# Linear attention and a top-1 expert layer on one core: two halves of a tile get PSUM banks of their own, a transpose moves from TensorE to VectorE, and four smaller edits

## The chip, the core and the metric

The kernel runs on one core of one Trainium2 chip. The metric is the device time of one execution in microseconds (us). TensorE multiplies and transposes into PSUM; VectorE (DVE), ScalarE (ACT) and GpSimd (POOL) work element by element; SyncE (SP) only issues transfers, and ACT issues a few too. Each engine runs its own instructions strictly in order, and an instruction starts when the semaphores that it waits for have reached their values.

## The reference

```python
def phi(x):                                   # 128 random features
    proj = np.einsum('bhsd,md->bhsm', x, omega)
    h = proj - np.sum(x * x, axis=-1, keepdims=True) / 2.0
    return np.exp(h - np.max(h, axis=-1, keepdims=True)) / np.sqrt(m)
q_p, k_p = phi(q_s), phi(k_s)                 # 4 batches, 8 heads, 576 rows, 64 columns
kv = np.einsum('bhsm,bhsd->bhmd', k_p, v); z = np.sum(k_p, axis=2)
x = np.einsum('bhsm,bhmd->bhsd', q_p, kv) / (np.einsum('bhsm,bhm->bhs', q_p, z)[..., None] + 1e-06)
# x as 2304 rows of 512; then a top-1 expert layer, 8 experts, at most 576 rows each
logits = x @ w_gate; e = argmax(logits); gate = softmax(logits)[e]
y[e] = relu(rows_of_e @ w1[e]) @ w2[e]        # 512 -> 1024 -> 512
out[i] = gate[i] * y[e][place of i]           # 0 where row i found no place
```

## The kernel before

**The attention.** The k phase has 18 steps n. Each projects 4 key units (`pjk`, line 172, TensorE), takes their maxima (`mx`, line 189, DVE), and makes the exponentials of the first half of the step on ACT out of PSUM (`ex`, line 794) and those of the second half by a DVE add (line 800) and an ACT exponential (line 803). Two steps later TensorE adds `ex` times v into `kacc` or `kp` (line 239). In step n=1 both halves lie in one tile of two banks (`x = pair("pjk1")`); from n=2 on each half has a bank of its own. When a batch's half is complete, the generator `kv_gate` copies it out, transposes it with two small pairs of TensorE transposes (`ktr`, line 264), which take the bank called SM, copies them on ACT (`kvT`, line 268) and multiplies by the gate weights (line 277). Its `yield "E"` hands over to the end of the running step.

**The q phase** has 18 tiles t and three steps behind them: project (`pjq`), subtract the maxima (`d`: ACT lines 809 and 827, POOL line 813), transpose (`qtr`, line 763), exponentiate (`qpT`, ACT line 819), multiply by kv (`qacc`, line 648), divide on DVE (`normalise`) and store the rows to the scratch tensor `x_d`. In steps 5 to 8 the transposes of the first 256 rows of expert item 0 (`xtri`, bank SM) run between those of `qtr`.

**The expert items.** A block of 576 rows goes through one expert: `mm1` for each of 8 column blocks f and two halves (rows 0 to 255, rows 256 to 575) with 12 matmuls in high and low parts (lines 689 to 691), evacuated by ACT (`hhi`, line 696; `hf`, line 698) and DVE (`hlo`, line 699) out of three banks in turn; then `mm2_rest` for the last 64 rows and `mm2` for four tiles of 128 rows (lines 866 to 868), `finish` (scale by the gate on ACT, line 896) and `put`, the store to `out` (line 930). `put` issues four of an item's five stores from SP and the last, the fourth 128-row tile, from ACT. Item 0 always runs; of the others, behind branches, items 1 and 2 run with this data, and item 3 does not. The rows of a later item and its w1 are loaded by `prefetch` in the item before, its w2 after the item's first `mm1`. Rows of items 1 and 2 are turned by a DVE transpose in `turn_x` (lines 402 to 406). Rows 256 to 575 of item 0 are instead turned by TensorE in three groups (line 412), one ahead of each of the last three half-0 column blocks f = 3, 4, 5, each followed by an ACT cast (line 422) and a DVE subtract (line 424).

**What sets the order.** Each engine's instructions stand in the order of the code; tiles in rotating buffers make the waits. All plain transfers go through eight counting semaphores, named DMAHW0 to DMAHW7 in the orders below.

Of the kernel before, what the change touches and what calls it, by code (L numbers as in the profile page):

```python
# [9 lines left out]
F32 = mybir.dt.float32  # L10
# [12 lines left out]
NT = N // 128  # L23
# [40 lines left out]
def attention_moe(ctx, tc, kT, qT, va, om, wg, w1, w2, cap, ident, tri, desc, lst, tab0, out):  # L64
# [183 lines left out]
    def kv_gate(b, g, acc):  # L248
        kv = kv_sb[b][:, 4 * g : 4 * g + 4, :]
        yield "E"  # L250
        nc.vector.tensor_copy(kv[:, :, 0:VW], acc[:, 0 : 4 * VW].rearrange("p (h c) -> p h c", h=4))
        kvc = small.tile([128, 2 * M], F32, tag="kvc", name=f"kvc{b}{g}", bufs=2)
        nc.scalar.copy(kvc.rearrange("p (h c) -> p h c", h=4), kv[:, :, 0:D])
        yield "E"
        kvT = small.tile([128, 2 * M], F32, tag="kvT", name=f"kvT{b}{g}", bufs=2)

        for a in range(2):
            f = slice(64 * a, 64 * a + 64)
            tr = []

            def small_t():
                tr.append(bank(SM, f"ktr{b}{g}{a}"))
                for i in range(2):
                    nc.tensor.transpose(tr[0][:, i * 64 : (i + 1) * 64], kvc[f, i * M : (i + 1) * M], id_sb[f, f])

            beside.append((a, small_t))
            yield "T"
            nc.scalar.copy(
                kvT.rearrange("p (i m) -> p i m", i=2)[:, :, f], tr[0][:, 0:128].rearrange("p (i m) -> p i m", i=2)
            )  # L270
        yield "T"
# [12 lines left out]
        yield "E"  # L284
        nc.vector.tensor_copy(kv[:, :, VW:ROW], sm[:, 0 : 4 * E].rearrange("p (h c) -> p h c", h=4))
# [33 lines left out]
    def setup():  # L319
# [5 lines left out]
        yield from pause(12)  # L325
        nc.vector.tensor_copy(cap_f, cap_i[:, 0:1])
        nc.vector.tensor_copy(tri_b, tri_sb)
        nc.vector.memset(ones_b, 1.0)
        nc.gpsimd.memset(sc_b, 0.0)
# [36 lines left out]

    def load_w(i, c, ev, chunks_of="(k p)"):
        if i == 1:
# [24 lines left out]

    def load_x(row):
        src = x_d[ds(row, SLOTS), :].rearrange("(b r) (q c) -> q r b c", r=32, q=4)
        for q in range(4):
            nc.sync.dma_start(big["xz"][32 * q : 32 * q + 32, :, :], src[q])


    def turn_x(b0, b1):  # L400
        t = big["xt"][:, 0 : b1 - b0, :].rearrange("p b (k r) -> p b k r", k=4)
        nc.vector.transpose(t, big["xz"][:, b0:b1, :].rearrange("p b (a k) -> p b k a", k=4))
        t = t.rearrange("p b k r -> p k b r")
        hi, lo = (big[x][:, :, 32 * b0 : 32 * b1].rearrange("p k (b r) -> p k b r", r=32) for x in ("xhi", "xlo"))
        nc.scalar.copy(hi, t)
        nc.vector.tensor_tensor(lo, t, hi.bitcast(F32), op=ALU.subtract)

# [231 lines left out]
    def first_rows():  # L639
        nc.sync.dma_start(  # L640
            big["xg"][:, 2:, :], x_d[2 * SUB : NSUB * SUB, :].rearrange("(i p) d -> p i d", p=SUB)
        )

# [14 lines left out]
    def normalise(t, acc):  # L658
        xr = small.tile([128, ROW, H], F32, tag="xr", name=f"xr{t}", bufs=4)
        if t < 2:  # L660
            xr_l[t] = xr
        av = acc.rearrange("p (i x) -> p i x", i=2)[:, :, 0 : NP * ROW].rearrange("p i (h c) -> p c i h", c=ROW)
# [10 lines left out]
        nc.vector.tensor_reduce(lg[:, t, :], xr[:, D + 1 : ROW, :], op=ALU.add, axis=AX.X)  # L673
        nc.sync.dma_start(x_d[t * 128 : (t + 1) * 128, :], xr[:, 0:D, :].rearrange("p c h -> p (c h)"))

    HALVES = [(0, 256), (256, SLOTS)]
# [42 lines left out]
    for n in range(NK + NT + 3):  # L719
# [3 lines left out]
        if n < NK:  # L723
# [6 lines left out]
            else:  # L730

                x = pair(f"pjk{n}") if n == 1 else None
                pj = [bank(2 * (n % 2) + i, f"pjk{n}{i}") if n > 1 else x[:, 512 * i : 512 * i + 512] for i in range(2)]
                project(keys, pj)
# [7 lines left out]
        if 0 <= t - 2 < NT:  # L742
# [7 lines left out]
            if t in FIRST_AT:  # L750
# [3 lines left out]
                rows = slice(64 * i, 64 * i + 64)  # L754
                x0 = xr_l[k0 // 2][:, 0:D, :].rearrange("p c h -> p (c h)")
                parts[i][0:0] = [
                    (tr[:, k * 64 : (k + 1) * 64], x0[rows, k * 128 : (k + 1) * 128], i) for k in range(4)
                ]
# [47 lines left out]
        else:  # L806
# [15 lines left out]
            if t >= NT:  # L822

                take()
            if t < NT:
                for k in range(4):
# [4 lines left out]
            if 0 <= t - 3 < NT:  # L831
                normalise(t - 3, acc_l[0])
                if t == 3:
                    start(first_item())
            run(times=3)
        if 0 <= t < NT and t - QB[c] == 2 and c + 2 < len(QB) - 1:
# [50 lines left out]

    def finish(i, pt, nm, scale, put):
        n = sub_n[i]
        y = hpool.tile([SUB, DM], F32, tag="y", name=f"ys{nm}{i}", bufs=3)  # L890
        src = pt
        if n < SUB:
            src = y
            nc.scalar.copy(y[0:n, :], pt[n : 2 * n, :])
            nc.vector.tensor_tensor(y[0:n, :], pt[0:n, :], y[0:n, :], op=ALU.add)
        nc.scalar.mul(y[0:n, :], src[0:n, :], scale[0:n])
        put(i, n, y)

# [18 lines left out]
    def item(j):  # L917
# [8 lines left out]

        def put(i, n, y, out_j=out_j):

            k = int(i == NSUB - 2)
            (nc.sync, nc.scalar)[k].dma_start(out_j[k][i * SUB : i * SUB + n, :], y[0:n, :])  # L930

        def prefetch():
# [4 lines left out]
            row = nc.sync.value_load(resd[0:1, 1, j : j + 1], min_val=0, max_val=N - S)  # L937
            load_x(row)
            for c in range(4):
                load_w(1, c, ev, "(p k)")  # L940
            evs.append(ev)
# [3 lines left out]
        for k, (f, half) in enumerate(STEPS[j > 0]):  # L945

            if j == 0 and k < 3:
                for _ in transpose_x(2 + k, nm, (SM, 3, None)[k]):
                    pass
            mm1(f, half, hhi, hlo, hf, nm)()  # L950
            if j == 0:

                listing(5 if k > 2 else 1)
            if j > 0 and k == 0:
                for c in range(4):
# [15 lines left out]
        for n, i in enumerate((NSUB - 1, *range(NSUB - 1))):  # L971
            pt = mm2(i, hhi, hlo, nm) if n > 0 else mm2_rest(hf, nm)
            finish(i, pt, nm, sc[:, i : i + 1], put)
            yield

            if not last:
                if n == 1:
                    turn_x(0, NBA)
                for c in ((), (0,), (1,), (), ())[n]:
                    split_w_hi(1, c)  # L980
                    split_w_lo(1, c)
                if n == 2:
                    turn_x(NBA, NB)

# [63 lines left out]

    def put_rows(i, n, y):
        scatter(out, idx[0:n, i, 0:1], y[0:n, :], N - 1)  # L1050
# [8 lines left out]
    with ExitStack() as ifs:  # L1059
# [5 lines left out]
        for j in range(J):  # L1065
# [5 lines left out]
            for c in range(4):  # L1071
                load_w(1, c, ev)
            for c in range(4):
# [81 lines left out]
```

## Time and profile before

| what | value |
|---|---|
| median of 3 runs | 266.65 us (265.68 to 266.78) |
| profiled execution, its own time | 265.75 us |
| span of its profile | 263.9 us, so 1.85 us lie outside the span |
| TensorE busy in the span | 254.9 us, 97% |
| DVE, ACT, POOL busy | 163.5, 149.0 and 36.7 us |
| granted TensorE clock | 0.994 of full speed |

The profiled execution is 0.9 us below the median. The busy share of TensorE is an average: it does not tell in which stretch it waits, so the stretches around each edit have to be read one by one.

### The profile page before, as it was taken

The page shows a single profiled execution, that of the slowest core. Times are in us where ns is not written, and L with a number is a line of the kernel's source. Part 1 is how long each engine was busy: PE and PEld are TensorE (multiplying, and loading weights), DVE is VectorE, ACT ScalarE, POOL GpSimd, SP SyncE. Part 2 cuts the span into 40 slices and gives each one's busy share as a digit, 9 for nine tenths or more (in the row PEclk, how much of TensorE's full clock was granted, in tenths as well). Part 3 has the DMA queues.
Part 4 walks back from the last instruction along what each step waited for, and adds up shares of the span by engine and source line. Part 5 has one row for each costly group of instructions (what it writes and reads, how often), then busy time and mean ns, then how long its engine had stood idle before and what let it go on. Part 6 is the DMA issues. An engine that isn't in the chain of part 4 may idle for free.

```text
span 263.9 us, 7550 instructions
## 1 busy us (share of the span) xinstructions
PE 254.9 (97%) x3070; PEld 226.6 (86%) x3070; DVE 163.5 (62%) x327; ACT 149.0 (56%) x375; POOL 36.7 (14%) x54
## 2 busy tenths in 40 slices
PE   7899999999999999999999999999999999999991
PEld 6789999999899999999868789996788999958880
DVE  3899888779989985745764725553337064633550
ACT  4688887999989993436413415552252255424321
POOL 2010000333469893000000000000000000000000
PEclk9999999999999999999999999999999999999997
DMA  7999760045867667791079439990011999101111
GB/s 226 390 383 330 273 230 2 5 156 166 275 214 234 248 251 260 256 387 67 2 144 292 170 87 348 190 283 1 21 42 48 292 263 298 36 2 53 46 42 45
DMA packets 33187, 46.56 MB, mean 176 GB/s; under 512 B 2227, under 2 KB 22067, under 8 KB 33139
## 3 DMA queue, kind: packets, MB, share of 16 engines
q1 hardware_dynamic: 32018, 44.42, 53.6%
q10 hardware_dynamic: 1120, 1.52, 1.7%
q8 instruction: 28, 0.46, 0.7%
q14 instruction: 21, 0.16, 0.2%
HBM read 34.00 MB, written 11.93 MB: 174 GB/s over the span
## 4 chain that ended last, share of the span: by engine, by line
PE 85%; DVE 5%; DMA 3%; ACT 2%; issue 2%; DVEq 0%
PE hi L689 10%; PE hi L690 10%; PE hi L691 10%; PE yi L866 8%; PE yi L867 8%; PE yi L868 8%; PE qacc L648 6%; PE pjq L172 5%; PE pjk L172 5%; DVE mx L189 3%; PE kacc L239 3%; DMA qraw<-qT 3%; PE kp L239 3%; PE qtr L763 3%; DVE ex L800 1%
## 5 line engine op out<-in xcount | busy, mean ns | idle before, releaser
L689 PE MATMUL hi<-xhi,w1hi 128*128 128x256 f32 (+1 forms) x192 | 57.1, 297 | 0.0
L690 PE MATMUL hi<-xhi,w1lo 128*128 128x256 f32 (+1 forms) x192 | 56.4, 294 | 0.0
L691 PE MATMUL hi<-xlo,w1hi 128*128 128x256 f32 (+1 forms) x192 | 56.3, 293 | 0.0
L699 DVE SCALAR_TENSOR_TENSOR hlo<-hi,hhi 128x256 fp32r<-128x256 f32 x48 | 20.2, 421 | 40.8 <-ACT hf L698 22.6
L696 ACT ACTIVATE hhi<-hi 128x256 fp32r<-128x256 f32 x48 | 18.5, 385 | 37.2 <-PE hi L691 37.2
L866 PE MATMUL yi<-w2hi,hhi 128*128 128x512 f32 x96 | 37.8, 393 | 0.1
L867 PE MATMUL yi<-w2hi,hlo 128*128 128x512 f32 x96 | 37.4, 389 | 0.0
L868 PE MATMUL yi<-w2lo,hhi 128*128 128x512 f32 x96 | 37.4, 389 | 0.0
L689 PEld LDWEIGHTS hi<-xhi,w1hi 128*128 128x128 f32 x192 | 36.0, 188 | 0.4
L690 PEld LDWEIGHTS hi<-xhi,w1lo 128*128 128x128 f32 x192 | 36.0, 188 | 0.1
L691 PEld LDWEIGHTS hi<-xlo,w1hi 128*128 128x128 f32 x192 | 36.0, 187 | 0.0
L813 POOL TENSOR_TENSOR d<-d,mx 128x512 f32<-128x512 f32 x18 | 18.7, 1041 | 53.1 <-DVE mx L189 49.6
L189 DVE TENSOR_REDUCE mx<-pjk 128x4 f32<-128x512 f32 (+1 forms) x38 | 23.3, 653 | 4.5 <-PE pjk L172 3.2
L866 PEld LDWEIGHTS yi<-w2hi,hhi 128*128 128x128 f32 x96 | 18.0, 188 | 6.5 <-issue 2.9
L794 ACT ACTIVATE ex<-pjk,mx 128x128 f32<-128x128 f32 x72 | 20.7, 369 | 4.8 <-DVE mx L189 4.6
L172 PE MATMUL pjk<-om_s,kraw 64*128 64x128 f32 x288 | 22.6, 287 | 0.7 <-DMA kraw<-kT 0.5
L648 PE MATMUL qacc<-kv_sb,qpT 128*64 128x73 f32 x576 | 22.4, 229 | 0.2 <-DVE e L601 0.2
L172 PE MATMUL pjq<-om_s,qraw 64*128 64x128 f32 x288 | 21.3, 284 | 0.5 <-DMA qraw<-qT 0.4
L868 PEld LDWEIGHTS yi<-w2lo,hhi 128*128 128x128 f32 x96 | 18.0, 188 | 3.8
L648 PEld LDWEIGHTS qacc<-kv_sb,qpT 128*64 128x64 f32 x576 | 19.8, 136 | 1.6 <-PE qtr L763 0.3
L867 PEld LDWEIGHTS yi<-w2hi,hlo 128*128 128x128 f32 x96 | 18.0, 188 | 3.6
L827 ACT ACTIVATE d<-pjq,mx 128x128 f32<-128x128 f32 x72 | 21.1, 405 | 0.1
(141 smaller groups left out, 399.4 us busy)
## 6 DMA issues: line engine op xcount, KB each, us to landing
w1raw<-w SPq DMA_DIRECT2D x16, 512.0 KB, 8.2
w2raw<-w SPq DMA_DIRECT2D x12, 512.0 KB, 4.9
qraw<-qT SPq DMA_DIRECT2D x6, 768.0 KB, 6.8
x_d<-xr SPq DMA_DIRECT2D x18, 256.0 KB, 3.2
v<-va SPq DMA_DIRECT2D x7, 650.0 KB, 6.7
xg<-x_d SPq DMA_DIRECT2D x12, 288.0 KB, 7.2
out<-zero_sb SPq DMA_DIRECT2D x4, 768.0 KB, 6.4
kraw<-kT SPq DMA_DIRECT2D x5, 576.0 KB, 6.5
```

The costliest lines, as they stand in the source:

```text
L172: nc.tensor.matmul(banks[i][:, k * M : (k + 1) * M], parts[k][rows, :], om_s[rows, :], start=True, stop=True)
L189: nc.vector.tensor_reduce(mx[:, a : a + src.shape[1]], src, op=ALU.max, axis=AX.X, negate=True)
L648: nc.tensor.matmul(acc[r : r + 64, i * 512 + p * ROW : i * 512 + (p + 1) * ROW], qpT[:, r // 64, (4 * i + p) * 64 : (4 * i + p) * 64 + 64] ...
L689: nc.tensor.matmul(pt, whi_[:, k, fs], xhi[:, k, sl], start=(k == 0), stop=False)
L690: nc.tensor.matmul(pt, wlo_[:, k, fs], xhi[:, k, sl], start=False, stop=False)
L691: nc.tensor.matmul(pt, whi_[:, k, fs], xlo[:, k, sl], start=False, stop=(k == 3))
L699: nc.vector.scalar_tensor_tensor(hlo[:, f, sl], pt[:, 0:w], 0.0, hhi[:, f, sl].bitcast(F32), op0=ALU.max, op1=ALU.subtract)
L794: nc.scalar.activation(ex[:, o + k, :], q[0][:, k * M : (k + 1) * M], AF.Exp, bias=mx[:, o + k : o + k + 1], scale=1.0)
L827: nc.scalar.activation(d[:, 4 + k, :], pj[1][:, k * M : (k + 1) * M], AF.Identity, bias=mx[:, 4 + k : 5 + k], scale=1.0)
L866: nc.tensor.matmul(pt, hhi[:, f, sl], w2hi, start=(f == 0), stop=False)
L867: nc.tensor.matmul(pt, hlo[:, f, sl], w2hi, start=False, stop=False)
L868: nc.tensor.matmul(pt, hhi[:, f, sl], w2lo, start=False, stop=(f == 7))
```

## The change

1. `kv_gate`: one more `yield "E"`; the transposes, copies and gate matmuls of each batch half come one step later.
2. `setup`: two small casts and a memset go from DVE to POOL.
3. w1 of item 0 is loaded in the other chunk order, POOL copies the first two `normalise` results into the buffer `xt` in that order, and the extra transposes of the q phase read `xt`.
4. Rows 256 to 575 of item 0 are loaded by four transfers in the layout of `turn_x` and turned by two DVE transposes of 128x640 in steps t=18 and 19, each followed one step later by an ACT cast and a POOL subtract of 128x4x160. The three groups of TensorE transposes, ACT casts and DVE subtracts are gone.
5. In step n=1 the first half goes to the bank SM, the second to the first bank of the pair.
6. The w2 of item 3 is loaded in item 2 behind its second store; the w2 loads of items 0 to 2 stay.
7. `finish` scales the fourth tile in two halves of 256 columns, and `put` stores the first half from SP, the second from ACT.

```diff
@@ kv_gate
         nc.scalar.copy(kvc.rearrange("p (h c) -> p h c", h=4), kv[:, :, 0:D])
         yield "E"
+        yield "E"
@@ setup
-        nc.vector.tensor_copy(cap_f, cap_i[:, 0:1])
-        nc.vector.tensor_copy(tri_b, tri_sb)
-        nc.vector.memset(ones_b, 1.0)
+        nc.gpsimd.tensor_copy(cap_f, cap_i[:, 0:1])
+        nc.gpsimd.tensor_copy(tri_b, tri_sb)
+        nc.gpsimd.memset(ones_b, 1.0)
@@
-    def load_w(i, c, ev, chunks_of="(k p)"):
+    def load_w(i, c, ev, chunks_of="(p k)"):
@@
-    def load_x(row):
-        src = x_d[ds(row, SLOTS), :].rearrange("(b r) (q c) -> q r b c", r=32, q=4)
+    def load_x(rows, b0=0):
+        src = x_d[rows, :].rearrange("(b r) (q c) -> q r b c", r=32, q=4)
         for q in range(4):
-            nc.sync.dma_start(big["xz"][32 * q : 32 * q + 32, :, :], src[q])
+            nc.sync.dma_start(big["xz"][32 * q : 32 * q + 32, b0:, :], src[q])
-    def turn_x(b0, b1):
-        t = big["xt"][:, 0 : b1 - b0, :].rearrange("p b (k r) -> p b k r", k=4)
+    def turn_x(b0, b1, o=0, eng=nc.vector):
+        t = big["xt"][:, o : o + b1 - b0, :].rearrange("p b (k r) -> p b k r", k=4)
         nc.vector.transpose(t, big["xz"][:, b0:b1, :].rearrange("p b (a k) -> p b k a", k=4))
...
-        nc.scalar.copy(hi, t)
-        nc.vector.tensor_tensor(lo, t, hi.bitcast(F32), op=ALU.subtract)
+        def split():
+            nc.scalar.copy(hi, t)
+            eng.tensor_tensor(lo, t, hi.bitcast(F32), op=ALU.subtract)
+
+        return split
@@ first_rows
-        nc.sync.dma_start(
-            big["xg"][:, 2:, :], x_d[2 * SUB : NSUB * SUB, :].rearrange("(i p) d -> p i d", p=SUB)
-        )
+        load_x(slice(32 * NBA, SLOTS), NBA)
@@ normalise
+        if t < 2:
+            xr_l[t] = big["xt"][:, 4 * t : 4 * t + 4, :]
+            nc.gpsimd.tensor_copy(xr_l[t], xr[:, 0:D, :].rearrange("p c h -> p (c h)").rearrange("p (m k) -> p k m", k=4))
@@ the k phase
-                x = pair(f"pjk{n}") if n == 1 else None
-                pj = [bank(2 * (n % 2) + i, f"pjk{n}{i}") if n > 1 else x[:, 512 * i : 512 * i + 512] for i in range(2)]
+                if n == 1:
+                    pj = [bank(SM, "pjk10"), pair("pjk11")[:, 0:512]]
+                else:
+                    pj = [bank(2 * (n % 2) + i, f"pjk{n}{i}") for i in range(2)]
@@ the q phase
+            if t > NT:
+                split_x()
...
+            if t in (NT, NT + 1):
+                b0 = NBA + 5 * (t - NT)
+                split_x = turn_x(b0, b0 + 5, b0 - NBA, nc.gpsimd)
@@ finish
-        nc.scalar.mul(y[0:n, :], src[0:n, :], scale[0:n])
-        put(i, n, y)
+        w = DM // parts
+        for c in range(0, DM, w):
+            nc.scalar.mul(y[0:n, c : c + w], src[0:n, c : c + w], scale[0:n])
+            put(i, n, y, c, w)
@@ put
-            k = int(i == NSUB - 2)
-            (nc.sync, nc.scalar)[k].dma_start(out_j[k][i * SUB : i * SUB + n, :], y[0:n, :])
+            k = int(i == NSUB - 2 and c > 0)
+            (nc.sync, nc.scalar)[k].dma_start(out_j[k][i * SUB : i * SUB + n, c : c + w], y[0:n, c : c + w])
@@ item
-            if j == 0 and k < 3:
-                for _ in transpose_x(2 + k, nm, (SM, 3, None)[k]):
-                    pass
-            if j > 0 and k == 0:
+            if 0 < j < B - 1 and k == 0:
                 for c in range(4):
                     load_w(2, c, evs[-1])
-            finish(i, pt, nm, sc[:, i : i + 1], put)
+            finish(i, pt, nm, sc[:, i : i + 1], put, 1 + (i == NSUB - 2))
             yield
+                if j == B - 2 and n == 1:
+                    for c in range(4):
+                        load_w(2, c, evs[-1])
```

The orders of the two programs at the three places that matter most follow. First DVE, from the first maxima of step n=1 (`mx_172`) into step n=2; before:

```order
L189 TENSOR_REDUCE mx_172<-pjk_173 128x4 [waits PE_49]
L189 TENSOR_REDUCE mx_172<-pjk_173 128x4 [waits Activation_49]
L800 TENSOR_TENSOR ex_182<-pjk_173,mx_172 128x512 [waits DVE_49]
L189 TENSOR_REDUCE mx_191<-pjk_192 128x4 [waits PE_49]
L189 TENSOR_REDUCE mx_191<-pjk_193 128x4
```

and of the change (`pjk_173` and `pjk_174` are now two tiles):

```order
L189 TENSOR_REDUCE mx_172<-pjk_173 128x4 [waits PE_49]
L189 TENSOR_REDUCE mx_172<-pjk_174 128x4
L807 TENSOR_TENSOR ex_183<-pjk_174,mx_172 128x512 [waits DVE_49]
L189 TENSOR_REDUCE mx_192<-pjk_193 128x4 [waits PE_49]
L189 TENSOR_REDUCE mx_192<-pjk_194 128x4
```

The wait of the second maxima for ACT is gone. Second, TensorE in item 0, from the last q result (`qacc`) into the column block f=3, before:

```order
L648 MATMUL qacc_2291<-kv_sb_75,qpT_2264 64x73 x14
L412 MATMUL xtri_2331<-id_sb,xg 128x128 [waits DMAHW5_49]
L412 MATMUL xtri_2331<-id_sb,xg 128x128 x3
L689 MATMUL hi_2338<-xhi,w1hi_1003 128x256
L690 MATMUL hi_2338<-xhi,w1lo_1007 128x256
L691 MATMUL hi_2338<-xlo,w1hi_1003 128x256
```

and of the change:

```order
L651 MATMUL qacc_2301<-kv_sb_75,qpT_2271 64x73 x14
L694 MATMUL hi_2343<-xhi,w1hi_995 128x256
L695 MATMUL hi_2343<-xhi,w1lo_999 128x256
L696 MATMUL hi_2343<-xlo,w1hi_995 128x256
L694 MATMUL hi_2343<-xhi,w1hi_995 128x256
```

The transposes ahead of f=3 are gone; those ahead of f=4 and f=5 are gone in the same way. Third, SP and ACT at the end of item 1, where the last tiles are stored and SP goes on to load the w2 of item 2. SP before:

```order
L930 DMA out<-ysi_8474 128x512 [waits DMAHW7_49,DMAHW0_49,Activation_49]
L930 ISA
L930 DMA out<-ysi_8507 128x512 [waits DMAHW1_49,DMAHW0_49,Activation_49]
L1095 COMPARE_AND_BRANCH
L372 ISA
L372 DMA w2raw_1010<-w 128x2x512 [waits DMAHW3_49,DVE_49,PE_49]
```

and of the change:

```order
L945 DMA out<-ysi_8500 128x512 [waits DMAHW5_49,DMAHW4_49,Activation_49]
L945 ISA
L945 DMA out<-ysi_8528 128x256 [waits DMAHW6_49,DMAHW5_49,Activation_49]
L1110 COMPARE_AND_BRANCH
L373 ISA
L373 DMA w2raw_1002<-w 128x2x512 [waits DMAHW0_49,DVE_49,PE_49]
```

The store of the first column half (`ysi_8528`) now stands ahead of the loads of w2. It reports on DMAHW6. ACT at the same place before:

```order
L896 ACTIVATE ysi_8507<-yi_8482,sc_j 128x512 [waits DMAHW6_49,PE_49,Activation_49]
L896 ACTIVATE ysi_8535<-yi_8510,sc_j 128x512 [waits DMAHW7_49,PE_49,Activation_49]
L930 ISA
L930 DMA out<-ysi_8535 128x512 [waits DMAHW1_49,DMAHW0_49,Activation_49]
L1095 COMPARE_AND_BRANCH
```

and of the change:

```order
L911 ACTIVATE ysi_8528<-yi_8503,sc_j 128x256 [waits DMAHW3_49,PE_49,Activation_49]
L911 ACTIVATE ysi_8528<-yi_8503,sc_j 128x256
L945 ISA
L945 DMA out<-ysi_8528 128x256 [waits DMAHW5_49,DMAHW6_49,DMAHW4_49,Activation_49]
L1110 COMPARE_AND_BRANCH
```

The second half's store on ACT waits for DMAHW6, the landing of the first half's store. The same pair stands at the end of item 2, the last that runs; in item 0 the ACT store waits for no store.

## Rows read from the trace of the kernel before

**Rows 1.** The page: span; busy time of the engines.

```profile
span 263.9 us, 7550 instructions
...
PE 254.9 (97%) x3070; PEld 226.6 (86%) x3070; DVE 163.5 (62%) x327; ACT 149.0 (56%) x375; POOL 36.7 (14%) x54
```

**Rows 2.** Waits of TensorE, whole run: us in total, times, longest.

```profile
PE pjk L172 <- DMA kraw<-kT: 0.5, 2, 0.3
...
PE qacc L648 <- DVE e L601: 0.2, 1, 0.2
```

**Rows 3.** Timeline from 7 us: start, length, instruction, [idle before <-releaser].

```profile
7.56 1.15 PE L239 MATMUL kacc<-v,ex 128*64 128x65 f32 x32
...
8.87 0.69 DVE L189 TENSOR_REDUCE mx<-pjk 128x4 f32<-128x512 f32 x1 [1.21 <-ACT ex L794]
...
10.11 0.44 PE L239 MATMUL kacc<-v,ex 128*64 128x130 f32 x4
...
11.00 1.14 PE L239 MATMUL kacc<-v,ex 128*64 128x130 f32 x28 [0.44 <-ACT ex L803]
...
11.51 0.69 DVE L800 TENSOR_TENSOR ex<-pjk,mx 128x512 f32<-128x512 f32 x1
...
12.35 1.16 PE L172 MATMUL pjk<-om_s,kraw 64*128 64x128 f32 x16 [0.21 <-DVE ex L800]
```

**Rows 4.** Timeline of ACT, then of TensorE, around 60 us.

```profile
57.88 0.37 ACT L268 COPY kvT<-ktr 128x128 f32<-128x128 f32 x1
...
59.47 1.29 ACT L827 ACTIVATE d<-pjq,mx 128x128 f32<-128x128 f32 x4
...
60.58 0.22 PE L763 MATMUL xtri<-id_sb,xr 64*128 64x64 f32 x1
```

**Rows 5.** Timeline of TensorE, 105.5 to 115 us.

```profile
105.78 1.25 PE L648 MATMUL qacc<-kv_sb,qpT 128*64 128x73 f32 x32
...
106.96 0.66 PE L412 MATMUL xtri<-id_sb,xg 128*128 128x128 f32 x4
...
107.57 0.28 PE L690 MATMUL hi<-xhi,w1lo 128*128 128x256 f32 x1
...
108.75 0.28 PE L691 MATMUL hi<-xlo,w1hi 128*128 128x256 f32 x1
...
112.72 0.31 PE L689 MATMUL hi<-xhi,w1hi 128*128 128x320 f32 x1
```

**Rows 6.** Groups by line and shape: busy us, mean ns of one, idle before.

```profile
L813 POOL TENSOR_TENSOR d<-d,mx 128x512 f32<-128x512 f32 x18 | 18.7, 1041 | 53.1 <-DVE mx L189 49.6 <-DVE e L607 1.8 <-DVE den L664 1.6
...
L140 POOL TENSOR_TENSOR w1lo<-w1raw,w1hi 128x256 fp32r<-128x256 f32 x16 | 11.4, 736 | 0.2
...
L402 DVE STREAM_TRANSPOSE xt<-xg 128x1280 f32<-128x1280 f32 x3 | 7.3, 2434 | 0.0
```

**Rows 7.** Timeline of ACT at the end of the run.

```profile
258.25 0.69 ACT L896 ACTIVATE ysi<-yi,sc_j 128x512 f32<-128x512 f32 x1 [3.81 <-issue]
258.97 0.35 ACTq L930 DMA_DIRECT2D out<-ysi  x1
```

**Rows 8.** Timeline of SP, ACT and TensorE at the start of item 2.

```profile
204.20 2.30 SPq L372 DMA_DIRECT2D w2raw<-w  x4
...
209.14 0.39 ACT L696 ACTIVATE hhi<-hi 128x256 fp32r<-128x256 f32 x1 [1.14 <-PE hi L691]
...
211.64 0.31 PE L689 MATMUL hi<-xhi,w1hi 128*128 128x320 f32 x1
...
217.16 1.05 ACT L137 CAST w2hi<-w2raw 128x1024 fp32r<-128x1024 f32 x1
```

**Rows 9.** DMA issues, 203 to 204.1 us: KB, us to landing.

```profile
out<-ysi SPq DMA_DIRECT2D x1, 256.0 KB, 2.1
```

**Rows 10.** DMA issues, 254 to 255 us.

```profile
out<-ysi SPq DMA_DIRECT2D x1, 256.0 KB, 3.3
```

**Rows 11.** DMA issues, 207.95 to 208.1 us.

```profile
out<-ysi ACTq DMA_DIRECT2D x1, 256.0 KB, 6.9
```

More of the change, by code (lines that the diff above doesn't have):

```diff
@@ L659, in normalise @@
         xr = small.tile([128, ROW, H], F32, tag="xr", name=f"xr{t}", bufs=4)
-        if t < 2:
-            xr_l[t] = xr
         av = acc.rearrange("p (i x) -> p i x", i=2)[:, :, 0 : NP * ROW].rearrange("p i (h c) -> p c i h", c=ROW)
@@ L754, in attention_moe @@
                 rows = slice(64 * i, 64 * i + 64)
-                x0 = xr_l[k0 // 2][:, 0:D, :].rearrange("p c h -> p (c h)")
+                x0 = xr_l[k0 // 2]
                 parts[i][0:0] = [
-                    (tr[:, k * 64 : (k + 1) * 64], x0[rows, k * 128 : (k + 1) * 128], i) for k in range(4)
+                    (tr[:, k * 64 : (k + 1) * 64], x0[rows, k, :], i) for k in range(4)
                 ]
@@ L886, in mm2_rest, with finish @@
         return pt
-    def finish(i, pt, nm, scale, put):
+    def finish(i, pt, nm, scale, put, parts=1):
         n = sub_n[i]
@@ L925, in item, with put @@
         sc = sc_b[:, 0, :] if j == 0 else sc_j[:, j - 1, :]
-        def put(i, n, y, out_j=out_j):
-            k = int(i == NSUB - 2)
-            (nc.sync, nc.scalar)[k].dma_start(out_j[k][i * SUB : i * SUB + n, :], y[0:n, :])
+        def put(i, n, y, c, w, out_j=out_j):
+            k = int(i == NSUB - 2 and c > 0)
+            (nc.sync, nc.scalar)[k].dma_start(out_j[k][i * SUB : i * SUB + n, c : c + w], y[0:n, c : c + w])
         def prefetch():
@@ L937, in prefetch @@
             row = nc.sync.value_load(resd[0:1, 1, j : j + 1], min_val=0, max_val=N - S)
-            load_x(row)
+            load_x(ds(row, SLOTS))
             for c in range(4):
-                load_w(1, c, ev, "(p k)")
+                load_w(1, c, ev)
             evs.append(ev)
@@ L972, in item @@
             pt = mm2(i, hhi, hlo, nm) if n > 0 else mm2_rest(hf, nm)
-            finish(i, pt, nm, sc[:, i : i + 1], put)
+            finish(i, pt, nm, sc[:, i : i + 1], put, 1 + (i == NSUB - 2))
             yield
             if not last:
+                if j == B - 2 and n == 1:
+                    for c in range(4):
+                        load_w(2, c, evs[-1])
                 if n == 1:
-                    turn_x(0, NBA)
+                    turn_x(0, NBA)()
                 for c in ((), (0,), (1,), (), ())[n]:
@@ L982, in item @@
                 if n == 2:
-                    turn_x(NBA, NB)
+                    turn_x(NBA, NB)()
     J = NJ
@@ L1047, in make_lists, with put_rows @@
         nc.vector.tensor_copy(res[:, 0, 15:16], inc[:, E - 1 : E])
-    def put_rows(i, n, y):
+    def put_rows(i, n, y, c, w):
         scatter(out, idx[0:n, i, 0:1], y[0:n, :], N - 1)
@@ L1071, in attention_moe @@
             for c in range(4):
-                load_w(1, c, ev)
+                load_w(1, c, ev, "(k p)")
             for c in range(4):
```

## The prediction

> **What bounds the kernel now.** I read the page first: TensorE is busy 97% of the span [rows 1], so the question is not which engine is full but where TensorE still waits, and what work of its own can go. The table of waits names the few places where TensorE stands still inside the run [rows 2]. It is short: most of what it lacks lies at the beginning and at the very end, where no matmul is left. So I read next the timeline of the first 14 us, where the reader is to see DVE waiting 1.21 us for ACT in the middle of step n=1 [rows 3], then the stretch in which item 0 starts, where TensorE transposes between the column blocks [rows 5], and last the tail, where one ACT instruction and one store stand alone behind the last matmul [rows 7]. An edit elsewhere moves the end only if TensorE waits for it.
>
> **The two banks of step n=1.** DVE's second maxima wait until 8.87 for the exponentials that ACT makes from the other half of the same tile, and ACT's reading has nothing to do with DVE's half. TensorE delivered both halves before it began the `kacc` group at 7.56. With two tiles the wait goes, so DVE is up to 1.2 us earlier from there [rows 3]. Does TensorE follow? Its next group of 32 starts at 10.11; 28 of them wait for ACT's exponential, which follows DVE's add, until 11.00, and end at 12.14. A group of 32 that does not wait takes 1.15, as the one at 7.56, so it would end at 11.26: 0.88 less. The projection behind it waits 0.21 more, for DVE's add that ends at 12.20; that add is 1.2 earlier too. Together 1.09 on TensorE. A small wait for a `kvc` copy in the next steps, which the later `kv_gate` takes away, can add a little; beyond 1.21 there is nothing to give. I take **-1.15**; bounds 0 (a transfer holds TensorE instead) and -1.3.
>
> **Item 0 without TensorE's transposes.** The last q result starts at 105.78, the transposes at 106.96, and the first half-1 block at 112.72 [rows 5]. Between the rows at 107.57 and 108.75 lie 10 matmuls, 0.118 each. The three blocks are 36 matmuls, 4.25 us; put at 106.96 they end at 111.21, which is **1.5** earlier. I take -1.45, for a hand-over from one block to the next, and -1.1 as the weak bound. What must be ready by 111.2 is the turned half: half a 2434 ns transpose is 1.22 us for each part on DVE [rows 6]. The second part stands in step t=19; even if it began only when the last q result is through, at 107.03, it would end at 108.25. The ACT cast is one pass over the same 640 columns; given as much as the transpose it ends at 109.5. The POOL subtract has no row of its own: 256 columns take 736 ns and 512 take 1041 ns on POOL [rows 6], so 640 take about 1.2 (estimate), and it ends at 110.7. So it is covered, with 0.5 us to spare in that worst order; a subtract of double length would cost 0.7. The Trainium skill (GPSIMD Engine Reference, section 3.1) gives two-input operations on GpSimd at half of VectorE's speed, 4497 ns for 2048 columns, which is an estimate of 1.4 us here; and its section 1 says that the two share their SBUF interfaces, so that DVE work with two SBUF inputs holds GpSimd up. By its speed alone the sum would not move; the sharing is a rival below.
>
> **The later gates.** One wait of 0.2 of the `qacc` group for DVE [rows 2] may go. But the last gate's second transposes now fall into step t=5, in which the extra transposes of item 0 use the same bank. Those must wait for ACT's `kvT` copy, and it stands behind four `d` instructions that end at 59.47 + 1.29 = 60.76; with a copy of 0.37 the bank is free at 61.13, where the transposes started at 60.58 before: up to +0.55 [rows 4]. As one such copy less stands ahead of these `d` instructions, ACT may get there 0.37 earlier. I take **+0.15**, bounds -0.3 and +0.6.
>
> **The fourth tile in two parts.** Here the order of the program speaks against the edit. Before, one ACT instruction of 0.69 starts at 258.25 and one store is issued at 258.97 [rows 7]; the span ends at 263.9 [rows 1], 4.93 after that issue. Now the first half is ready about 0.4 after 258.25 (estimate: half of 0.69 and a start), and SP issues it at about 258.65. The second half on ACT waits until the first has landed. A store of 256 KB from SP into a quiet queue lands after 2.1 [rows 9], so ACT issues at about 260.75, 1.8 later than before. Half the bytes may shorten the two landings by some tenths; no row shows a store of this shape. I take **+1.6**, bounds +1.2 and, if the first half lands in 3.3 as the third tile of item 2 did [rows 10], +2.8. The Trainium skill (DMA: Bandwidth & Descriptors, section on the anatomy of one DMA) gives a transfer a fixed part of about 2.0 us, mostly the confirmation at the target, and 436 KB per us on top; two stores in a row by that (estimates of 2.3 each against one of 2.6) would make the tail 1.7 longer, and the sum about -0.75 in place of -0.85.
>
> At the end of item 1 the same pair stands. ACT is then held until about 207.7 + 2.1 = 209.8 and a further 0.4 for its own issue, so the first `hhi` of item 2, at 209.14 before, comes at about 210.2; it and its `hlo` take some 0.8, to 211.0. TensorE enters that bank again at 211.64 [rows 8]: no cost up to a landing of about 2.7, and from there one for one. SP's loads of item 2's w2, issued from 204.20 before, now stand behind the first half's store and go out at about 208.3; even at the slowest landing of a store in that traffic, 6.9 [rows 11], w2 is there by 215.2, and ACT casts it at 217.16 [rows 8]: no cost. In item 0 no such wait exists.
>
> **At nothing.** The casts and the memset moved to POOL, and the two POOL copies of 128x512, lie on an engine that is busy 36.7 us of 263.9 [rows 1]; the copies must be through before step 5, some 1.0 each by the POOL row of that width [rows 6]. The chunk order of w1 moves no byte more. The w2 of item 3 is loaded though item 3 does not run: 2 MB in item 2, beside which only its stores run; the third tile's store may queue behind it, and the next one that waits for that comes about 6 us later.
>
> **The sum.** -1.15 - 1.45 + 0.15 + 1.6 = **-0.85** on the profiled execution's 265.75, which makes 264.9. That execution lies 0.9 below the median of 266.65; on the median it is 265.8. I forecast **265.7**, and count anything within 0.5%, 1.33 us, as no change, since the three runs shown differ by 1.1. Its own range, with each term some tenths off, is 265.0 to 266.5.
>
> **The rivals.**
> - *The second half's store costs nothing* (chance 0.18). If the first half lands well before the second is ready, or the wait is satisfied early, the tail is as before or some tenths shorter: -2.5 in the sum, 264.2. For it: the halves are small. Against it: every store of 256 KB shown takes 2.1 or more, the second half is ready 0.4 after the first.
> - *The bank gain does not arrive* (0.12). TensorE waits twice for `kraw` in the first steps [rows 2]; if such a landing takes the place of the ACT wait, the first term is 0 and the sum +0.3: 266.95. Against it: the waits named are 0.3 and 0.2 long, and the group that gains waits for ACT and DVE alone.
> - *Slower: the wait at the end of item 1 reaches TensorE* (0.12). If the first half's store lands as late as ACT's store did at the same place, 6.9 [rows 11], ACT is held until 214.6, and issue, `hhi` and `hlo` end at about 215.8: TensorE stands 4.1 us, the sum is +3.3, 269.9. It decides at a landing of 2.7; to make the kernel slower beyond the bound it has to pass 4.9. Against it: the loads that slowed that store now stand behind it on SP.
> - *GpSimd late* (0.03). If DVE's work holds the subtract, so that TensorE waits 1.5 us at the first half-1 block, the second term is gone: 267.2.
>
> **How the numbers follow.** The forecast has 0.55; of it about 0.12 lies beyond -1.33. Faster: 0.12 + 0.18 = 0.30. Slower: 0.12. The rest, 0.43 + 0.12 + 0.03 = 0.58, is no change. The range 264.0 to 267.3 takes in the first two rivals and the fourth and leaves out the slower one.
>
> **What would show it.** In the changed trace: no wait of DVE for ACT near 7.7, and the projection of step 4 near 11.3; the first half-1 block 1.5 nearer to the last q result; the extra transposes of t=5 waiting for ACT; and in the tail ACT's store 2 us behind SP's, the span's end 6.5 us behind the last matmul group's ACT work. The forecast is wrong if ACT's last store goes out before 260, if TensorE waits for `xlo` or for a bank at the start of item 2, or if it meets a transfer near 11 us.

## The result, and the profile after

The change ran in 262.81 us (262.63 to 262.9) beside 266.71 us of the kernel before (265.68 to 267.03): ratio 0.987, 95% interval 0.983 to 0.991. Timed again on another chip it gave 263.47 beside 265.75 us, 0.992 (0.989 to 0.994). It is faster, by 2.3 to 3.9 us, and lies below the range that was given. The profiled execution has a span of 261.1 us, 2.8 less than before [rows 1].

Each term of the sum is read from the distance between two fixed points of the two traces: the starts of a projection step, of a column block or of the last matmul, the last landing, the span's end.

| stretch | forecast, us | from the traces, us |
|---|---|---|
| start of k step n=3 | none | +0.18 |
| from there to the start of step 6 (banks) | -1.15 | -1.28 |
| from there to q step 7 (gates, extra transposes) | +0.15 | +0.35 |
| q steps 7 to 9 (a q load) | none | -0.50 |
| item 0 up to its half-1 blocks (transposes) | -1.45 | -1.41 |
| rest of item 0 | none | -0.34 |
| start of item 2 | 0 | +0.21 |
| last matmul to last landing (two-part store) | +1.6 | +1.49 |
| last landing to the end of the span | 0 | -1.46 |
| sum | -0.85 | -2.76 |

The page of the changed kernel, engines as in [rows 1]:

```profile
span 261.1 us, 7559 instructions
...
PE 253.9 (97%) x3058; PEld 226.7 (87%) x3058; DVE 164.1 (63%) x323; ACT 149.3 (57%) x377; POOL 42.6 (16%) x61
```

TensorE is as full as before, with 12 instructions less. Its waits in the changed kernel (us in total, times, longest):

```profile
PE wps L301 <- DVE warm L295: 1.2, 1, 1.2
PE xtri L770 <- ACT kvT L269: 0.3, 1, 0.3
```

The wait of `qacc` [rows 2] is gone, and the one for `kvT` is the wait that the later gate was forecast to bring. It is met in q step 5, in the timeline of TensorE (start, length, instruction, [idle before <-releaser]):

```profile
59.80 0.24 PE L770 MATMUL xtri<-id_sb,xt 64*128 64x64 f32 x1 [0.27 <-ACT kvT L269]
```

The timeline from 7 us, to be read beside [rows 3]:

```profile
7.35 1.29 DVE L189 TENSOR_REDUCE mx<-pjk 128x4 f32<-128x512 f32 x2 [0.20 <-PE pjk L172]
8.07 1.14 ACT L801 ACTIVATE ex<-pjk,mx 128x128 f32<-128x128 f32 x4 [0.47 <-DVE mx L189]
...
9.20 1.16 PE L172 MATMUL pjk<-om_s,kraw 64*128 64x128 f32 x16
...
10.29 1.36 PE L239 MATMUL kacc<-v,ex 128*64 128x130 f32 x32
...
11.59 1.16 PE L172 MATMUL pjk<-om_s,kraw 64*128 64x128 f32 x16
```

DVE takes both maxima without a stop, the `kacc` group is no longer cut in two, and step 4 starts 2.39 behind step 3, where it was 3.33. That is 0.94 of the 1.28; the other 0.34 lies between steps 4 and 6, where TensorE waited for the `kvc` copy before (0.2 in its table of waits) and no longer does. Where the change turns the rows of item 0, the timelines of TensorE and then of POOL show:

```profile
105.71 0.39 PE L694 MATMUL hi<-xhi,w1hi 128*128 128x256 f32 x1
...
110.06 0.31 PE L694 MATMUL hi<-xhi,w1hi 128*128 128x320 f32 x1
```

```profile
103.27 1.56 POOL L409 TENSOR_TENSOR xlo<-xt,xhi 128x640 fp32r<-128x640 f32 x1 [3.44 <-ACT xhi L408]
106.66 1.57 POOL L409 TENSOR_TENSOR xlo<-xt,xhi 128x640 fp32r<-128x640 f32 x1 [1.83 <-ACT xhi L408]
```

Nothing stands between the column blocks any more; the first half-1 block, at 112.72 before [rows 5], comes at 110.06, and the second subtract is through 1.83 earlier, at 108.23. ACT at the start of item 2, beside [rows 8]:

```profile
204.31 0.84 ACT L911 ACTIVATE ysi<-yi,sc_j 128x256 f32<-128x256 f32 x2 [3.82 <-issue]
206.68 0.45 ACTq L945 DMA_DIRECT2D out<-ysi  x1
207.85 0.66 ACT L701 ACTIVATE hhi<-hi 128x256 fp32r<-128x256 f32 x2 [2.70 <-PE hi L696]
```

ACT waits for the landing of SP's half, which takes 1.70, and the first `hhi` comes 1.7 later than the shift of 3.0 would put it. The issue of ACT's store at the same place before, just ahead of the `hhi` of [rows 8]:

```profile
208.03 0.38 ACTq L930 DMA_DIRECT2D out<-ysi  x1
```

From the start of that issue to `hhi` at 209.14 ACT needs 1.11 before, and 1.17 in the change: the issue takes 0.4, and a branch and the load of a register lie behind it. The tail, where [rows 7] stood:

```profile
254.99 0.39 PE L881 MATMUL yi<-w2lo,hhi 128*128 128x512 f32 x1
255.47 0.84 ACT L911 ACTIVATE ysi<-yi,sc_j 128x256 f32<-128x256 f32 x2 [3.81 <-issue]
255.97 0.33 SPq L945 DMA_DIRECT2D out<-ysi  x1
258.31 0.35 ACTq L945 DMA_DIRECT2D out<-ysi  x1
```

The issues of transfers in the last 9 us, KB each and us to landing:

```profile
out<-ysi SPq DMA_DIRECT2D x1, 128.0 KB, 2.2
out<-ysi ACTq DMA_DIRECT2D x1, 128.0 KB, 1.7
```

The chain of two landings is there, as forecast. What is not as forecast is the end: the last landing is at 260.04, and the span ends 1.07 later. Before it was at 261.35, 2.53 ahead of the end. What SP does in that time are semaphore and branch instructions, which the views leave out; from the records of SP in the two packed traces (start, instruction):

```
before                                      after
261.36 .. 261.69  5 semaphore waits         256.86 .. 257.25  6 semaphore waits
261.76  branch                              257.32  branch
262.25 .. 262.94  12 semaphore waits        257.50 .. 259.31  9 semaphore waits
                                            260.06 .. 260.18  3 semaphore waits
263.01  drains, end at 263.88               260.25  drains, end at 261.12
```

Item 3 does not run, and the branch that skips it settles in SP the counts of the transfers that it would have issued. Before, these were 4 loads of w2 and 5 stores, 9 transfers, so all eight DMAHW semaphores had to be waited for, those of the last stores too. Now item 3 has six transfers left, on six semaphores, and the two last stores use the other two: SP goes through the branch and 9 of the 12 waits behind it before the last store has landed.

### The profile page after: what moved, and what is told of

It reads as the page before. It is cut to its first block, busy times and chain, and to the rows that moved or that the text cites. A ratio compares the mean times of both kernels' runs of the same rounds, so it can differ in the third digit from the quotient of the medians.

```text
span 261.1 us, 7559 instructions
## 1 busy us (share of the span) xinstructions
PE 253.9 (97%) x3058; PEld 226.7 (87%) x3058; DVE 164.1 (63%) x323; ACT 149.3 (57%) x377; POOL 42.6 (16%) x61
## 4 chain that ended last, share of the span: by engine, by line
PE 92%; ACT 3%; issue 2%; DVE 1%; ACTq 0%
PE hi L694 10%; PE hi L695 10%; PE hi L696 10%; PE yi L879 8%; PE yi L880 8%; PE yi L881 8%; PE pjk L172 8%; PE qacc L651 7%; PE pjq L172 6%; PE kacc L239 4%; PE kp L239 4%; PE qtr L770 3%; ACT d L836 1%; PE yi2r L891 1%; PE yi1r L891 1%
## 5 line engine op out<-in xcount | busy, mean ns | idle before, releaser
L172 PE MATMUL pjk<-om_s,kraw 64*128 64x128 f32 x288 | 23.3, 297 | 0.0
```

What stands on the lines that cost most here:

```text
L172: nc.tensor.matmul(banks[i][:, k * M : (k + 1) * M], parts[k][rows, :], om_s[rows, :], start=True, stop=True)
```

## The experiments

The first theory was that the transfer count of the skipped item hides SP's closing work, worth more than 1 us, and that the two-part store costs what was forecast; its rival, that the two-part store is free. Then came the gate, the banks and the setup instructions. The letters in the expectations name the theories that each weighs. "Tail" is the time from the start of the last matmul to the end of the span; it is 6.10 before and 6.13 after, and in two more executions of the change 5.68 and 6.08.

**The early w2 taken out of the change.**

```diff
-            if 0 < j < B - 1 and k == 0:
+            if j > 0 and k == 0:
...
-                if j == B - 2 and n == 1:
-                    for c in range(4):
-                        load_w(2, c, evs[-1])
```

> The changed kernel with the w2 of item 3 loaded in item 3 again, as before; everything else of the change stays. Theory A (the closing): item 3 is skipped, and its way around makes SP wait once for every semaphore that its transfers would have raised. With four w2 loads and the stores in it these are all eight, the last store's among them, so SP's closing work of about 1.6 us starts only after the last landing; without the loads it runs ahead of that landing. Then this kernel ends 2.5 us after its last landing instead of 1.1, and takes 262.8 + 1.45 = 264.2 to 264.4. Theory B (the halves): the tail is short because each half lands sooner; then the w2 loads play no part and the time stays 262.8.

264.54 us beside 265.89, ratio 0.996 (0.994 to 0.999). The end comes 2.33 behind the last landing, and the tail is 6.88.

**The early w2 alone, put into the kernel before** (the same lines the other way round).

> The kernel before with nothing but the w2 of item 3 loaded in item 2. Theory A (the closing): 1.45 less than the kernel before, about 265.2, with the span ending about 1.1 us after the last landing. Theory B (the halves): no change, 266.7.

263.9 beside 265.89, 0.993 (0.990 to 0.995), 2.0 less where theory A had 1.45. The end comes 0.94 behind the last landing, and the tail is 4.41 where it was 6.10. ACT and its one store stand behind the last matmul as in [rows 7], and 1.59 of the 1.69 are won behind the landing:

```profile
258.70 0.69 ACT L896 ACTIVATE ysi<-yi,sc_j 128x512 f32<-128x512 f32 x1 [3.81 <-issue]
259.42 0.35 ACTq L930 DMA_DIRECT2D out<-ysi  x1
```

So a load that no item uses takes closing work off the time behind the last landing: 1.26 with the two-part store (2.33 against 1.07), 1.59 without it.

**One store for the fourth tile, in the changed kernel.**

```diff
-            k = int(i == NSUB - 2 and c > 0)
+            k = int(i == NSUB - 2)
...
-            finish(i, pt, nm, sc[:, i : i + 1], put, 1 + (i == NSUB - 2))
+            finish(i, pt, nm, sc[:, i : i + 1], put)
```

> The changed kernel with the fourth tile scaled and stored in one part from ACT again; the early w2 load stays. Theory A (the closing): the two parts alone delay the last landing by about 1.5 us, and the early w2 load alone took 1.45 out of the closing; without the parts the kernel takes 262.8 - 1.5 = 261.3, and 0.2 less if the wait at the start of item 2 goes too: 261.1. Theory B (the halves): the parts make the tail short, and without them the time is 264.3 or at least 262.8.

261.53 beside 265.89, 0.985 (0.982 to 0.988); tail 4.74, and item 2 starts without the 0.21. And a second time:

> The changed kernel with the fourth tile stored in one part, a second time beside the change without the gate step: 1.2 to 1.6 less than the change, about 1.5% less than the kernel before.

261.48 beside 265.71, 0.984 (0.982 to 0.986); tail 4.51. The mean of the two tails is 1.3 below the mean of the three of the change. So the two-part store costs 1.3 at the end and 0.2 at the start of item 2: it brings the last landing about 1.5 later, and 0.2 come back behind the landing, where the end takes 1.07 with two parts and 1.26 with one. The change itself was not timed in these two comparisons; by its ratios in the two others the second store costs between 0.2% and 0.8%, 0.7 to 2.1 us. This kernel is the fastest of the study. The last issue and landing of its second profile, where the change has two in a row:

```profile
out<-ysi ACTq DMA_DIRECT2D x1, 256.0 KB, 2.1
```

**The change again, on another chip.**

> The change itself once more, beside the next three on one chip. The executions so far spread by up to 2.5 us, and their traces differ in the first 12 us, by when the second piece of the first keys lands (9.0 to 11.4). If that landing is the spread, this kernel spreads like the others and its median lies 2.5 to 3 us under that of the kernel before; if the added gate step is worth the 2.6 us by which the medians of the change and of the version without it differ, the median is 262.8 again and spreads little.

263.47 beside 265.75, 0.992 (0.989 to 0.994), 2.3 less. Its six executions lie between 262.13 and 264.10; that the four of the first comparison lay between 262.63 and 262.9 was luck.

**The two banks alone, on the kernel before** (part 5 of the diff).

> The kernel before with the two banks of step n=1 and nothing else. Theory E (the gain depends on when the keys land): from the start of the projection of step 3 to that of step 4 it takes 2.4 in place of 3.3 when the keys land at 9, and nothing is gained when they land at 11, where the kernel before takes 2.5 too; so between 0.2 and 1.1 less than before, about 0.6 in the median. Theory F (a full wait removed): 1.1 less whatever the landing.

265.47 beside 265.75, 0.999 (0.997 to 1.001). In the profile step 4 follows step 3 by 2.39, as in the change, and the k phase from step 3 to step 17 takes 33.89 where it took 35.06 before; but step 3 itself starts only at 10.61. The gain is in the trace, and the median, 0.28 less, does not show it apart from no change. Theory F, 1.1 less in every execution, is refuted: the interval ends at 0.74 less. For theory E speaks an execution without the banks in which step 3 starts late, the profile with the early w2 alone. DVE waits its 1.21 for ACT there too, and yet the `kacc` group behind step 3 is whole, because TensorE comes to it only at 12.14:

```profile
11.05 1.16 PE L172 MATMUL pjk<-om_s,kraw 64*128 64x128 f32 x16
12.14 1.36 PE L239 MATMUL kacc<-v,ex 128*64 128x130 f32 x32
```

From step 3 to step 6 it takes 7.43 there, 8.22 in the first profile of before, 8.04 in the second (below), 6.94 in the change and 6.95 with the banks alone. So the banks are worth between 0.5 and 1.3 us, by when the first keys land.

**The change without parts 2, 3 and 4** (TensorE turns the rows of item 0, the setup stays on DVE).

> The kernel before with the gate step, the two banks, the early w2 load and the two-part store, but item 0's rows still turned by TensorE from the old load. Expected by the sum: 1.4 more than the change on the same chip, all of it between the last q result and the first half-1 block, which is 6.4 in place of 5.0 from the start of the last q results to it. If the four smaller row loads or DVE's transposes cost something elsewhere, the difference is less than 1.2.

266.31 beside 265.75, 1.003 (1.001 to 1.005). From the third half-0 block to the first half-1 block it takes 8.50, the change 7.09: 1.41 for the transposes. A further 1.2 is lost between the k steps 7 and 12, where DVE's cast of `cap_f` waits 0.79 for its transfer. Together that is 2.6; the median lies 2.84 above that of the change on the same chip, where 1.4 was expected. The 1.2 is the setup, which the next kernel takes by itself.

**The setup instructions back on DVE, in the changed kernel.**

```diff
-        nc.gpsimd.tensor_copy(cap_f, cap_i[:, 0:1])
-        nc.gpsimd.tensor_copy(tri_b, tri_sb)
-        nc.gpsimd.memset(ones_b, 1.0)
+        nc.vector.tensor_copy(cap_f, cap_i[:, 0:1])
+        nc.vector.tensor_copy(tri_b, tri_sb)
+        nc.vector.memset(ones_b, 1.0)
```

> The changed kernel with the three small setup instructions on VectorE again, the rest of the change in place. Theory G (they guard the bank gain): the first of them waits for a small load that lands at 18.2 to 19.2 whatever VectorE does, and VectorE, 1.2 us earlier than before, reaches it at about 17 when the first keys land early; it then stands until that landing, 1 to 1.5 us, plus 0.5 of work, and TensorE behind it: 1 to 1.8 more than the change, and the projections of steps 7 to 12 lose it. Theory H (as predicted, they cost nothing either way): the same time as the change.

264.16 beside 265.71, 0.994 (0.992 to 0.997), where the change has 0.992 (0.989 to 0.994) on another chip: on these medians the move is worth about 0.7 us, and the intervals overlap. The timeline of DVE and a wait of TensorE in that profile:

```profile
18.57 0.15 DVE L327 CAST cap_f<-cap_i 128x1 f32<-128x1 int32 x1 [0.76 <-DMA cap_i<-cap]
18.65 0.22 DVE L328 CAST tri_b<-tri_sb 128x128 bf16<-128x128 f32 x1
18.84 0.17 DVE L329 MEMSET ones_b<- 128x128 bf16 x1
18.92 1.22 DVE L189 TENSOR_REDUCE mx<-pjk 128x4 f32<-128x512 f32 x2
```

```profile
PE ktr L265 <- ACT kvT L269: 1.0, 1, 1.0
```

The banks make DVE earlier, so that it reaches the cast before the transfer lands; the maxima stand behind the cast, and steps 7 to 12 take 13.34 where the change takes 12.27. That is theory G, with a wait of 0.76 in place of 1 to 1.5. It does not strike every execution: with the two banks alone, whose setup stands on DVE too, step 3 started late, DVE reached the cast just as its transfer landed, and steps 7 to 12 took 12.28:

```profile
18.71 0.15 DVE L326 CAST cap_f<-cap_i 128x1 f32<-128x1 int32 x1
```

In the change POOL meets the same transfer, with nothing urgent behind it:

```profile
18.21 0.19 POOL L327 CAST cap_f<-cap_i 128x1 f32<-128x1 int32 x1 [16.66 <-DMA cap_i<-cap]
```

**One gate step taken back, in the changed kernel** (the second `yield "E"` removed).

> The changed kernel without the added step in the gate generator. Theory C (the bank in step t=5 costs): the wait of the extra transposes for ACT's copy goes, and TensorE is 0.4 to 0.5 earlier in step t=6; a wait of 0.2 for DVE in step t=4 and one of 0.2 in the k phase come back, so 262.5 to 262.9. Theory D (the later gates are a gain): those two waits and a load of q that TensorE meets earlier cost more: 263.1 to 263.4.

265.41 beside 265.89, 0.998 (0.996 to 1.001), above what either theory allows. The same with the one store of the fourth tile:

> The changed kernel with the fourth tile stored in one part and without the added gate step. Theory C (the bank in step t=5 costs 0.25 over steps 3 to 9, all that the step does): 0.25 less than with the gate step, so 1.4 + 0.25 less than the change on the same chip. Theory D (the gate step is a large gain): 1 us or more above the change with one store.

262.47 beside 265.75, 0.987 (0.984 to 0.989). And again:

> The changed kernel without the added gate step, a second time, for another trace and for its median beside the others on one chip. Theory C (the step costs 0.25 in steps 3 to 9 and nothing else): at or slightly below the change. Theory D (the step is a gain that the first trace did not show): 1 to 2 us above it, with waits of TensorE for ACT or DVE in the k phase.

264.93 beside 265.71, 0.999 (0.997 to 1.002). So the step looked worth 1 to 2 us, against a forecast of +0.15. Three more profiles, with one of the change beside them, told part of where:

> The changed kernel without the added gate step, for a further trace. Its medians lie 1 to 2 us above the change, and its two traces show no such loss in the stages. Theory I (its slower executions lose in the k phase, where the gates meet late loads): a trace over 264 us shows waits of TensorE for ACT, DVE or a load before 48 us. Theory J (they lose behind it, in code that arrives late or in the last landing, by chance): the loss lies behind 100 us, as waits that end with nothing the profile shows.

> The same once more. Theory I: waits before 48 us. Theory J: waits of unseen cause behind 100 us, or a late last landing.

> The same once more. Theory I: waits before 48 us. Theory J: waits of unseen cause behind 100 us, or a late last landing.

> The change itself for a third trace on the same chip. Theory I: no waits of TensorE in the k phase, whatever the landing of the first keys. Theory J: the same kind of late waits as in the versions without the gate step, as often.

Single executions: 265.88, 265.21 and 263.57, the change 264.35, before 265.25. In the stages the step costs about what was forecast: from k step 3 to q step 9 it takes 61.87 with it and 61.62 without. But in all five profiles with the two-part store and without the step the last store lands 2.69 to 3.09 after its issue, and in the three of the change after 1.73. The DMA queues and the issues behind ACT's last issue, first in the third profile without the step, then in the change:

```profile
q10 hardware_dynamic: 144, 0.13, 12.5%
q8 instruction: 1, 0.02, 2.3%
q14 instruction: 1, 0.01, 0.9%
...
out<-ysi ACTq DMA_DIRECT2D x1, 128.0 KB, 3.0
```

```profile
q10 hardware_dynamic: 144, 0.13, 13.8%
q14 instruction: 1, 0.01, 1.2%
...
out<-ysi ACTq DMA_DIRECT2D x1, 128.0 KB, 1.7
```

The packet of q8 is 16 KB of code. It starts 0.71 behind the issue and takes 1.19. Of the store's 144 packets 135 have started by 1.37; the other nine, a sixteenth, start only from 1.90 on, when the code is through. So the share of one of the 16 DMA engines waits for it: 15 of the 16 updates arrive by 1.73, the last at 3.00. Without the step this load falls into the last store; in the kernels with it, and in those of before, the last load of q8 starts ahead of that store's issue, and then costs 0 to 0.3. In the five profiles it costs 1.0 to 1.4, as theory J has it. Beside it stand the spread of the start and waits of TensorE without a cause in the profile, of 0.3 to 0.5 in three of the six profiles of the changed kernel without the step. The sixth, with one store, has the extra load too, but it starts 2.51 behind the issue, when the store has landed (2.05); that kernel's median is nevertheless 0.5 to 1.0 above those with one store and the step (other chips, and the intervals overlap), and its profile has two such waits, 0.5 and 0.3. So the code load accounts for most of the loss with the two-part store; what the step changes to put the load there, and where the rest goes, stays open.

**Before once more.**

> The kernel before once more, for a second trace of it. If the spread of the executions lies in the landing of the first keys, in the wait for one load of q and in the last landing, this trace differs from the first in those three places and nowhere else by more than 0.3 us.

266.35 us, span 264.5. Step 3 starts at 10.71, not at 9.02, and the q load is not waited for. The 0.50 at q steps 7 to 9 is thus chance. So is, as far as these profiles go, the 0.34 in item 0: with the early w2 alone, which leaves item 0 as it is, its part from the first half-1 block on takes 43.08, where the first profile of before took 43.39 and this one 43.20. Over all profiles step 3 starts at 8.73 to 11.39. In the chain that ended last this is a transfer of the keys; in the second profile with one store:

```profile
3.10 6.96 DMA kraw<-kT
```

That is most of the 2.5 us by which executions of one kernel differ: in the three profiles of the change the start of step 3 moves by 1.93 and the time by 2.22.

## Why the prediction was wrong

**The step that failed is "At nothing".** Two edits that it priced at nothing move the time. With the first alone the sum of -0.85 becomes -2.31, which is 264.3 on the median. That the first comparison gave 262.81, below the range, has chance in it too (see what is left over).

*The w2 of item 3* was looked at as 2 MB of traffic that hides behind item 2. Its traffic did cost nothing: the store that queues behind it lands after 4.7 in place of 2.1, and holds no one. But the edit also takes four transfers out of the skipped item, and with them 1.46 us of SP's closing work off the path in the profile, 1.26 and 1.59 in the two experiments. The row for it was in the trace of before: between the landing of a store issued at 258.97 [rows 7] that takes 2.4 and the end at 263.88 lie 2.5 us, and the prediction took "4.93 after that issue" as one fixed block without asking what fills it.

*The setup instructions on POOL* were costed by POOL's spare time. What mattered is the engine that they left: in the two profiles with the gate step, the banks and the setup on DVE, DVE stood 0.76 and 0.79 at a transfer, and 1.07 and 1.2 of what the banks had won were lost. The sum came out right there by luck, since the bank term was priced as if nothing took it back.

**The other terms held in these two traces.** The banks gave 1.28 for 1.15, by the mechanism named: the wait of DVE is gone, the `kacc` group is whole, and the projection follows. The working had the group too short: the 1.15 at 7.56 is that of 32 matmuls of 65 columns, while 28 of 130 took 1.14 [rows 3], and the whole group takes 1.36. That left 0.94 at the group, for 1.09, and the wait for `kvc` made up for it. That both profiled executions had early keys is luck; with the latest keys of a kernel without the banks 0.5 of the gain is left. The transposes gave 1.41 for 1.45, and the row of the 10 matmuls of 0.118 was enough to size them. The POOL subtract took 1.56, not the 1.2 worked out from the neighbouring widths, but the second transpose came early and 1.83 was to spare. By the speed that the Trainium skill (GPSIMD Engine Reference, section 3.1) states, the estimate was 1.4; the two subtracts, at 1.56 and 1.57, are above that too. The gates cost 0.35 with the forecast wait of `xtri` in them. At the start of item 2 the landing took 1.70, below the 2.7 from which it was to cost, and yet TensorE lost 0.21; with one store the loss is gone, so the wait of ACT is its cause. The working counted 0.4 from ACT's issue to its first `hhi`, where the trace of before has 1.11; with these 0.7 the limit lies near 2.0, not at 2.7, and the rest of the difference stays open.

**The two-part store** cost 1.49 up to the last landing, for 1.6. ACT's store went out 2.34 behind SP's. The sign of being wrong "before 260" was met at 258.31 and says nothing: the first three terms, -2.45 together, already put the forecast's own 260.75 at 258.3. The end came 5.65 behind ACT's last scaling, as before (5.63): the two-part store and the closing cancel there. The halves landed after 2.2 and 1.7, and in the second profile of the change both after 1.7. The Trainium skill (DMA: Bandwidth & Descriptors, the anatomy of one DMA), which describes transfers that GpSimd issues, would give 2.3 for each (estimate); the 1.7 of these transfers, issued by SP and ACT, is below that and below its fixed part of 2.0.

**The rivals.** "The second half's store costs nothing" gives 264.2, the nearest of the times, but its mechanism did not happen: the store costs, and something else pays. "The bank gain does not arrive" happens in part where the keys land late. ACT's wait at item 2 took 0.2, not 4. GpSimd was not late.

**What is left over.** Of the 1.91 by which the two profiled executions beat the sum, 1.46 is the closing; 0.50 and 0.34 are not seen, or less, in the second profile of before and are put down to chance, with 0.18 of chance and the 0.21 at item 2 against them. On the medians the change gains 3.9 in the first comparison and 2.3 in the second; the first had four executions of each kernel, too few for a start that moves by 2.5: the kernel before has a median of 266.71 there and of 265.75 over the 23 of the second, the change 262.81 and 263.47. That the second lies so near the corrected sum of -2.31 is partly luck, since the banks alone gave 0.28 on the median.

## What to carry to other kernels

Ask of the time behind the last landing what fills it, and which engine's waits could run ahead of the landing: in this program a transfer in a branch that is skipped still has its semaphore settled there, and moving it out of the branch paid without its data being used. When a stall is taken away, look for what the earlier engine meets next, above all small instructions that wait for a late transfer and stand ahead of large ones. Two dependent stores in the tail cost most of a landing here: 1.3 us, for landings of 1.7 to 2.2.

## What the hardware showed unexpectedly

A code load of 16 KB goes through the same 16 DMA engines as the data and takes 0.96 to 1.27 us on one of them in the five profiles where it falls into the last store; the kernel ends 1.0 to 1.4 us later. The Trainium skill (Runtime: NRT & Kernel Launch, on instruction fetch) states that code is fetched in 16 KiB blocks by a DMA queue; the packets of q8 agree, those of q14 have 8 KB. The cost here is to the store beside the load. A last store of 128x256 with no load of q8 in it lands after 1.72 to 1.75, one of 128x512 after 2.05 to 2.4, and after 2.05 to 2.06 where code costs it nothing: half the bytes save 0.3. Taking out one `yield`, which moves the stages by 0.25, put such a code load into the last store in all five profiles with the two-part store; an edit of that kind is judged by its stages and by its tail apart.
